# The first 1.5 KB of every row of one value load, fetched by six small loads of their own

## The chip, the cores and the metric

The kernel runs on one core of one Trainium2 chip. The metric is the device time of one execution in microseconds (us). Three runs of the kernel before took 186.15, 186.21 and 186.29 us; the median is 186.21 us. The profile below is of one further execution, which took 186.22 us.

## The reference

One decoding step of grouped attention over a window of a cache. 32 requests (B) have one query token each, with 32 query heads of 128 numbers; 8 key and value heads each serve four query heads. Of 2048 cached positions only the last 512 are used.

```
q = x @ wq                                     # x 32 x 512, wq 512 x 4096
k, v = k_cache[:, :, 1536:, :], v_cache[:, :, 1536:, :]   # 32 x 8 x 512 x 128
p = softmax(q . k / sqrt(128))                 # per request and query head, over 512 positions
o = p . v                                      # 32 x 32 x 128
out = o.reshape(32, 4096) @ wo                 # wo 4096 x 512
```

All inputs are bf16. The parts of the two caches that are read have 33.5 MB each, the two weight matrices 4.2 MB each, so 75.5 MB have to be read for 32 KB of result.

## The kernel before

The 32 requests are worked off in eight quads q of four. One quad's keys are one load of 4 MB: 32 pairs of request and head, each cut into four runs of 128 positions, make 128 rows, one for each partition of the on-chip memory, and each row is one contiguous run of 32 KB in HBM (128 positions of 256 B). The values of a quad are laid out the same way. There are two buffers for keys (`K_sb`) and two for values (`V_sb`); quad q uses buffer q % 2. The weights have no room of their own: `wq` lies in the second value buffer until the queries are made, `wo` in the first key buffer when quad 6 has been transposed.

For each quad VectorE transposes the keys (T, L444, two halves), TensorE makes the scores (S, L331), VectorE and ScalarE make the softmax (M, X, N), TensorE turns the probabilities to the layout of the value rows (E, L346) and ScalarE copies them out (G), VectorE and ScalarE spread them into block-diagonal weights (B), TensorE multiplies them with the values (P, L361), both engines pick the wanted blocks (C), and TensorE folds them (F, L373), which ScalarE copies (D). At the end TensorE multiplies with `wo` (L392) in three parts, as its three loads W0 (16 of 32 column blocks), W1 (12) and W2 (4) come in; VectorE and ScalarE copy the result, and one write of 32 KB ends the program.

The order of the operations on TensorE, VectorE and ScalarE is written out by hand (`PE_OPS`, `DVE_OPS`, `ACT_OPS`); each waits for what `needs` lists. The order of the loads is the list `LOADS`. All of them but those of `x` are issued by SyncE (SP), in this order:

```
K0 K1 V0.0 K2 V1.0 K3 V2.0 K4 V3.0 K5 K6 V4.0 K7 V5.0 V5.1 V6.0 V6.1 V7.0 V7.1 W0 W1 W2
```

The two loads of `wq` come ahead of this list. A load of keys waits until quad q - 2 has been transposed (L227), a load of values until quad q - 2 has been multiplied (L233), V1 until the queries are made (L231). `V_PIECES` says in how many loads a quad's values come: one for quads 0 to 4 and two (V5.0 and V5.1) for 5 to 7. Each load of values adds 16 to a semaphore of its buffer and piece (`sem_v`); `v_waits` (L178) works out what count TensorE has to wait for before it multiplies with a piece, from all loads that have used that semaphore so far.

The four loads of `x` are issued by ScalarE's queue. They have 2, 6, 10 and 14 rows of 1 KB (`X_PARTS`).

## Time and profile before

| what | measured |
|---|---|
| median of three runs | 186.21 us |
| the profiled execution | 186.22 us |
| its span, first to last instruction | 184.4 us |
| outside the span | 1.8 us |
| bytes read, mean rate over the span | 75.53 MB, 410 GB/s |
| TensorE busy (matmul), VectorE busy, ScalarE busy | 119.1, 106.6, 49.9 us |
| SP issues W2, W2 has landed | 157.82, 181.40 us |
| the last matmul has ended, the write is issued | 181.86, 182.53 us |

The profile is a page on one execution; its trace can be asked for more: for the chain of work that ended last, for the waits, for the instructions in a stretch of time, and for the transfers in it. Data come over 16 DMA engines that work beside each other. A load is cut into packets, here one for each row and engine, and each engine that took part in a load adds to the load's semaphore by a 4-byte packet after its last row. The "DMA" row of the page is the mean busy share of the 16 engines in each slice. Queue q1 is SP's, q10 ScalarE's; the "instruction" queues fetch the program itself. The trace also keeps each packet's start, length and size and the time of each semaphore addition, but not the number of the engine that moved it.

### The profile page before, as it was taken

The numbers are of one execution on the slowest core, as the hardware profiler recorded it, in microseconds if no ns is written. First come the engines' busy times: TensorE is split into PE (matmuls) and PEld (weight loads), VectorE is DVE, ScalarE is ACT, GpSimd is POOL, SyncE is SP. The second block draws the span as 40 slices with busy tenths as digits, with TensorE's granted clock in tenths as the row PEclk, the third lists the DMA queues.
The fourth block names the chain that finished last, engine by engine and source line by source line (L and its number), as shares of the span: only waits on it lengthen the run. The fifth ranks groups of instructions, "written<-read, shape, count | busy, mean of one in ns | idle before, by whom it ended". The sixth has DMA issues, their size and how long they took to land.

```text
span 184.4 us, 3662 instructions
## 1 busy us (share of the span) xinstructions
PE 119.1 (65%) x1636; PEld 56.8 (31%) x1636; DVE 106.6 (58%) x106; ACT 49.9 (27%) x93; POOL 16.9 (9%) x52
## 2 busy tenths in 40 slices
PE   0089104448796794549944992441799899988872
PEld 0024000014542451304431450000245445444362
DVE  0032999994549632963298327999636996302031
ACT  3001200011935157001650162001062714502031
POOL 7900040202000200002000200020000000000000
PEclk9999955555599999657987699555579999999999
DMA  6999999989999999998999999999999999999970
GB/s 224 412 508 398 398 455 455 455 384 412 451 455 437 398 409 455 455 430 377 435 451 455 412 405 434 441 448 405 434 430 402 430 426 423 426 419 430 422 314 32
DMA packets 3584, 75.80 MB, mean 411 GB/s; under 512 B 432, under 2 KB 496, under 8 KB 624
## 3 DMA queue, kind: packets, MB, share of 16 engines
q1 hardware_dynamic: 3504, 75.53, 96.1%
q8 instruction: 13, 0.21, 0.5%
q10 hardware_dynamic: 64, 0.03, 0.1%
q14 instruction: 3, 0.02, 0.0%
HBM read 75.53 MB, written 0.03 MB: 410 GB/s over the span
## 4 chain that ended last, share of the span: by engine, by line
DMA 77%; DVE 13%; issue 3%; PE 3%; SPq 3%; DVEq 0%
DMA K_sb<-in_k_cache_dram 49%; DMA V_sb<-in_v_cache_dram 15%; DMA K_sb<-in_wo_dram 13%; DVE KT_sb L444 12%; PE ps L361 2%; SPq L236 1%; SPq L228 1%; SPq L242 1%; PE ps L331 1%; SPq L193 0%; DVE C_sb L469 0%; DVE maxv L450 0%; PE ps L392 0%; DVEq L120 0%; DVE P_bf L478 0%
## 5 line engine op out<-in xcount | busy, mean ns | idle before, releaser
L444 DVE STREAM_TRANSPOSE KT_sb<-K_sb 128x4096 f32<-128x4096 f32 x16 | 70.6, 4433 | 12.5 <-DMA K_sb<-in_k_cache_dram 12.4
L361 PE MATMUL ps<-V_sb,bd 32*128 32x512 bf16 x1024 | 63.3, 397 | 4.6 <-DMA V_sb<-in_v_cache_dram 2.7
L331 PE MATMUL ps<-KT_sb,QBD 128*32 128x512 bf16 x256 | 25.2, 532 | 39.7 <-DVE KT_sb L444 30.1
L361 PEld LDWEIGHTS ps<-V_sb,bd 32*128 32x128 bf16 x1024 | 27.1, 97 | 37.9 <-issue 12.2
L331 PEld LDWEIGHTS ps<-KT_sb,QBD 128*32 128x32 bf16 x256 | 6.6, 114 | 56.1 <-DVE KT_sb L444 37.0
L495 ACT ACTIVATE P_f<-ps,negmax 128x512 f32<-128x512 f32 x8 | 5.5, 687 | 63.2 <-DVE negmax L452 63.2
L508 ACT ACTIVATE bd<-PTc,mask 128x512 bf16<-128x512 bf16 x31 | 20.1, 710 | 0.3
L513 ACT ACTIVATE C_sb<-ps 32x512 f32<-32x512 f32 x22 | 12.9, 588 | 25.5 <-PE ps L361 25.4
L289 POOL COPY QBD<-QT_sb 32x128 bf16<-32x128 bf16 x32 | 9.2, 287 | 106.5 <-PE ps L331 90.3
L464 DVE TENSOR_SCALAR bd<-PTc,mask 128x512 bf16<-128x512 bf16 x33 | 9.4, 349 | 13.9 <-ACT PTc L502 13.9
L469 DVE COPY C_sb<-ps 32x512 f32<-32x512 f32 x10 | 6.9, 692 | 15.6 <-PE ps L361 15.5
L373 PE MATMUL ps<-C_sb,F_sb 128*128 128x128 f32 x64 | 9.7, 299 | 6.4 <-ACT C_sb L513 5.8
L346 PE MATMUL ps<-P_bf,E_sb 128*128 128x128 bf16 x128 | 11.0, 254 | 0.8 <-DVE P_bf L458 0.8
L373 PEld LDWEIGHTS ps<-C_sb,F_sb 128*128 128x128 f32 x64 | 8.2, 201 | 9.4 <-ACT C_sb L513 8.1
L346 PEld LDWEIGHTS ps<-P_bf,E_sb 128*128 128x128 bf16 x128 | 9.3, 116 | 4.9 <-DVE P_bf L458 2.8
L502 ACT ACTIVATE PTc<-ps 128x512 bf16<-128x512 f32 x8 | 4.8, 594 | 18.2 <-PE ps L346 18.1
L450 DVE TENSOR_REDUCE maxv<-ps 128x1 f32<-128x512 f32 x8 | 5.5, 687 | 7.2 <-PE ps L331 7.2
L313 PE MATMUL ps<-V_sb,bd 128*128 128x512 bf16 x32 | 8.6, 435 | 0.8 <-DVE bd L412 0.8
L301 PE MATMUL ps<-bd 32*128 32x128 bf16 x4 | 0.6, 295 | 9.0 <-DMA bd<-in_x_dram 9.0
L412 DVE CAST bd<-ps 128x512 bf16<-128x512 f32 x1 | 0.7, 692 | 9.6 <-PE ps L301 9.6
L433 DVE CAST KT_sb<-ps 128x512 bf16<-128x512 f32 x4 | 2.5, 684 | 6.0 <-PE ps L313 6.0
L489 ACT ACTIVATE KT_sb<-ps 128x512 bf16<-128x512 f32 x4 | 2.1, 602 | 13.8 <-PE ps L313 13.8
(29 smaller groups left out, 33.9 us busy)
## 6 DMA issues: line engine op xcount, KB each, us to landing
K_sb<-in_k_cache_dram SPq DMA_DIRECT2D x8, 4096.0 KB, 25.6
V_sb<-in_v_cache_dram SPq DMA_DIRECT2D x5, 4096.0 KB, 30.0
V_sb<-in_v_cache_dram SPq DMA_DIRECT2D x6, 2048.0 KB, 16.4
V_sb<-in_wq_dram SPq DMA_DIRECT2D x2, 2048.0 KB, 9.8
K_sb<-in_wo_dram SPq DMA_DIRECT2D x1, 2048.0 KB, 19.8
K_sb<-in_wo_dram SPq DMA_DIRECT2D x1, 1536.0 KB, 22.8
K_sb<-in_wo_dram SPq DMA_DIRECT2D x1, 512.0 KB, 23.6
out_dram<-P_bf SPq DMA_DIRECT2D x1, 32.0 KB, 1.5
```

The costliest lines, as they stand in the source:

```text
L289: pool.tensor_copy(QBD[pr, q % 2].rearrange("p (w t) (h c) -> p w t h c", w=2, h=HKV)[:, :, :, :, 4 * b:4 * b + 4], QT_sb[pr, q].rearrange ...
L313: ins = pe.matmul(ps[:, n], lhsT=xT_sb[:, kt, :], rhs=wq_sb[:, kt, n * 512:(n + 1) * 512], start=kt == 0, stop=kt == DKT - 1, tile_positio ...
L331: ins = pe.matmul(S_ps[32 * c:32 * c + 32, :], lhsT=QBD[:, q % 2, 2 * w + t, c0:c0 + 32], rhs=KT_sb[:, w, :, KB * h:KB * h + KB, t], start ...
L346: ins = pe.matmul(EP_ps[:, e * R:(e + 1) * R], lhsT=E_sb[:, k, e].rearrange("p m j -> p (m j)"), rhs=P_bf[:, k * R:(k + 1) * R], start=k = ...
L361: ins = pe.matmul(O_ps[:, b, :], lhsT=bd[pr, q % 2, 4 * g:4 * g + 4].rearrange("p r h e -> p (r h e)"), rhs=V_sb[q % 2][pr, 512 * g:512 * ...
L373: ins = pe.matmul(F_ps[:, 0:P], lhsT=F_sb[:, d].rearrange("p h d -> p (h d)"), rhs=C_sb[:, q % 2, :, 32 * d:32 * d + 32], start=d == 0, st ...
L444: return dve.transpose(KT_sb[:, w].bitcast(F32).rearrange("p r c t -> p r (c t)"), K_sb[q % 2][:, :].bitcast(F32).rearrange("p (r w c) -> ...
L450: dve.tensor_reduce(maxv[:, q:q + 1], S_ps, AX.X, ALU.max).then_inc(s["dve_m"], 1)
L464: ins = dve.tensor_scalar(o, i, m, None, op0=ALU.mult)
L469: ins = dve.tensor_copy(*pick_args(q, r))
L508: ins = act.activation(o, i, ACTF.Copy, scale=m)
L513: ins = act.activation(*pick_args(q, r), ACTF.Copy)
```

## The change

For the second quad (q = 1) the first 6 positions of each row's 128, which are 1.5 KB of its 32 KB, no longer come with the row. They come by six loads of their own, ahead of the row's rest, over the partitions of 6, 6, 6, 6, 5 and 3 pairs of request and head (24, 24, 24, 24, 20 and 12 partitions). The rest of each row, 30.5 KB, is one load over 128 partitions as before. All seven loads add to the same semaphore, so that `v_waits` counts six more for this buffer from quad 1 on. They are issued where V1 stood. The destination, the order of all other operations and the number of bytes are the same.

```diff
 V_PIECES = [1, 1, 1, 1, 1, 2, 2, 2]
+V_HEAD, V_HEAD_R = 1, 6
+V_HEAD_LOADS = [(0, 6), (6, 12), (12, 18), (18, 24), (24, 29), (29, 32)]
@@ v_waits
                     c = sum(1 for p in range(q % 2, q + 1, 2) if V_PIECES[p] > i)
+                    if i == 0 and q >= V_HEAD and q % 2 == V_HEAD % 2:
+                        c += len(V_HEAD_LOADS)
                     yield i * 32 // n, sem_v[q % 2][i], 16 * c
@@ the loads of values, on SP
                     n = R // V_PIECES[q]
-                    r0 = op[2] * n
+                    r0, r1 = op[2] * n, op[2] * n + n
+                    if q == V_HEAD:
+                        r0 = V_HEAD_R
+                        for w0, w1 in V_HEAD_LOADS:
+                            sp.dma_start(
+                                V_sb[q % 2][4 * w0:4 * w1, 0:r0 * DH],
+                                v_cache[4 * q:4 * q + 4, :, SK - W:, :].rearrange(
+                                    "b h (k r) d -> (b h) k (r d)", k=KB)[w0:w1, :, 0:r0 * DH],
+                            ).then_inc(sem_v[q % 2][0], 16)
                     sp.dma_start(
-                        V_sb[q % 2][:, r0 * DH:(r0 + n) * DH], rows(v_cache, q, r0, r0 + n)
+                        V_sb[q % 2][:, r0 * DH:r1 * DH], rows(v_cache, q, r0, r1)
                     ).then_inc(sem_v[q % 2][op[2]], 16)
```

## The prediction

> **What bounds the kernel now.** I read the slices and the queues of the page first, then the chain of work that ended last, then the transfers and the instructions of the last microseconds.

> ```profile
> DMA  6999999989999999998999999999999999999970
> GB/s 224 412 508 398 398 455 455 455 384 412 451 455 437 398 409 455 455 430 377 435 451 455 412 405 434 441 448 405 434 430 402 430 426 423 426 419 430 422 314 32
> q1 hardware_dynamic: 3504, 75.53, 96.1%
> q8 instruction: 13, 0.21, 0.5%
> q10 hardware_dynamic: 64, 0.03, 0.1%
> ```

> The sixteen DMA engines are busy from the first slice to the last but two, at some 425 GB/s. No compute engine comes near that. Each load is also issued well ahead: the tightest, V7.0, is issued at 155.49 us, when the foremost engine still has V6.1 to move until 158.6. So an engine's end is the sum of its packets. The chain's end says the same:

> ```profile
> 157.35 0.43 SPq L242
> 157.78 0.04 issue
> 157.82 23.57 DMA K_sb<-in_wo_dram
> 181.40 0.04 issue
> 181.44 0.42 PE ps L392 x15
> 181.86 0.02 issue
> 181.88 0.28 DVE P_bf L478
> ```

> The last part of `wo`, W2, lands at 181.40 us and 16 matmuls wait for it; from there to the end of the span it is a fixed 3.0 us. What counts is whether all engines end together. They don't. Time by stages, with the share of the sixteen engines that was busy and GB/s in the last two columns:

> ```profile
> 176.00:178.00 2.00, 1.40 (x12) 1.14 (x10) 0.72 (x2) 0.80 (x2) 0.00 (x0) 1.00 0.94 381
> 178.00:179.60 1.60, 1.17 (x65) 0.90 (x64) 0.00 (x0) 0.28 (x1) 0.00 (x0) 1.00 0.48 197
> 179.60:180.80 1.20, 0.60 (x44) 0.60 (x48) 0.00 (x0) 0.00 (x0) 0.00 (x0) 1.00 0.26 106
> ```

> From 179.6 to 180.8 us a quarter of the engines is at work: four, at the same 26.5 GB/s each that they have when all work (425 / 16), so it is the engine that limits and not what they share. The sixteen additions to W2's semaphore agree: twelve come between 178.26 and 180.05 us, then four at 181.19, 181.31, 181.37 and 181.40.

> What makes four late? In the packet records an engine can be followed, since its next packet starts 3 to 4 ns before the last one's end. A 16 KB row takes 607 ns from start to start, but a 16 KB piece of program (queue q8, for TensorE, one every 256 of its instructions) holds its engine for 1.55 us: 1.05 us until the next row starts and 0.5 us by which that row is longer. The pieces go to eight engines in turn, and by the end four engines have carried two: those fetched at 46.3 and 151.2, 57.3 and 161.0, 68.1 and 167.6, 81.5 and 176.7 us. These are the four.

> **Which engines a small load uses.** The loads of `x` have 2 + 6 + 10 + 14 = 32 rows, and q10 shows 64 packets: 32 rows and 32 additions, one for each engine that took part. So a load of n rows ran on n engines. Followed through, six engines carry at least three of these rows, four carry two, four one, two none, as if each load took the first n of one fixed order. Of the four late engines two carry two rows and two carry one. None is among the first six.

> **The change, part by part.**

> 1. The head loads' engines. The source of a head load is walked as 6 (or 5, or 3) heads, in each 4 runs. The rows bound it: 6 rows of `x` went to 6 engines, and loads over 128 partitions, whose source is walked as 32 heads of 4 runs, to all 16. I take the number of heads, 6, 6, 6, 6, 5, 3, by the row that it is nearest to, the 6-row load; the other end, with 24 partitions as the number that is divided, is 12 engines, a rival. [...]

> 2. What it takes off. Rows of 16 KB and 4 KB take 607 and 155 ns, which is 0.0368 ns a byte and 4 ns besides. A row that is 1536 bytes shorter saves 56.5 ns, and each engine has 8 of the 128 rows: 0.45 us off all sixteen, and off the ten beyond the first six for good. The four late ones then bring W2 at 181.40 - 0.45 = 180.95.

> 3. What it adds. A row of 1536 bytes costs 4 + 56.5 = 61 ns by that line, between the 46 ns of a 1 KB row of `x` and the 159 ns of a 4 KB row of W2; I take 61, as the 1 KB row lies on the line (42 ns from start to start). A load over 6 engines gives each 4 such rows. The first three engines get 24 rows and 6 additions of 6 ns: 1.46 + 0.04 - 0.45 = +1.04 us; the fourth and fifth 20 rows, +0.79; the sixth 16 rows, +0.54. Of those six the latest now (it carried one piece of program, at 142.5 us) brings W2 at 180.05, the next at 179.38. With +1.04 the latter comes to 180.42, which is early. The former comes to 180.59 if it is the sixth, 180.84 if the fourth or fifth, both under 180.95; if it is one of the first three, 181.09. The records don't tell which.

> 4. Six more issues on SP, some 0.57 us each by the rows of its 25 (0.37 to 0.62): 3.7 us. They stand where V1 stood, at 32.98 us, so the rest of V1 is issued at 36.7. Behind it SP waits for the transpose that releases K3 (42.23), so nothing behind is later. The engines come to V1 at about 51 us, when K2 is through. Without this cover it would cost 3.7 us.

> 5. V1's arrival. The last addition of V1 comes at 62.98 now, from a late engine, and goes to 62.5 there; the first six come at 61.3 to 61.7, and with +1.04 at 62.7 at most. TensorE starts on it at 63.11, after the scores of quad 3. Nothing waits longer. TensorE's wait counts seven loads instead of one in the same instruction, and its instruction count, and so its program fetches, stay.

> 6. The end. W1 (180.16) is late on the same four engines and moves by 0.45 as well, as does V7.1, on which the matmuls ahead wait. TensorE is idle for 0.67 us ahead of W1 and 0.38 us ahead of W2:

> ```profile
> 178.46 1.08 PE L392 MATMUL ps<-K_sb,o_sel 128*32 128x128 bf16 x64 [0.37 <-ACT o_sel L517]
> 180.20 0.85 PE L392 MATMUL ps<-K_sb,o_sel 128*32 128x128 bf16 x48 [0.67 <-DMA K_sb<-in_wo_dram]
> 181.44 0.43 PE L392 MATMUL ps<-K_sb,o_sel 128*32 128x128 bf16 x16 [0.38 <-DMA K_sb<-in_wo_dram]
> ```

> W0's matmuls end at 179.54 even without any shift and W1 is there at 179.71, so the whole 0.45 us passes to the end.

> The sum: 186.22 (the profiled execution, which is 0.01 us from the median) - 0.45 = 185.77 us, 0.24% less. The measurement tells about 0.2%, 0.37 us, from no change, so this is a narrow "faster".

> **The rivals.**

> A. The engine that brings W2 at 180.05 is one of the first three. Then it is the last, at 181.09, and the gain is 0.31 us: 185.91. For it: three of six places. Against it: nothing but the other three.

> B. The head loads spread over 12, 12, 12, 12, 10 and 12 engines. Then the two late engines in places seven to ten get 11 rows: 0.67 + 0.04 - 0.45 = +0.26 us, so W2 at 181.66 and 186.48 us, within 0.2%. Against it: the 6-row load of `x` on 6 engines.

> C. Slower: a 1.5 KB row costs more than its bytes, on the first three engines at 52 us. The point from which this decides: 180.05 - 0.45 + 24 c is later than 181.40 for c above 75 ns (102 ns if rival A's engine isn't among the three). At 4 KB's 159 ns W2 would come at 183.4 and the run end at 188.2; at 100 ns, at 182.0 and 186.8. For it: the 1 KB rows of the result took 45 to 79 ns. Against it: those run on idle engines with nothing behind them, while the rows of `x`, in a full queue as here, took 44 to 46. [...]

> D. Slower: in the new program the pieces of program go to other engines, and a twice-hit engine is among the first three. Then W2 comes at 181.40 + 1.04 and the run takes 187.26. Against it: TensorE's instructions stay, and three runs within 0.14 us don't look like a draw.

> E. Nothing at all, 186.21: some other thing holds the end.

> **How the numbers follow.** The likeliest gets 0.52 and A 0.25: by places alone they would share evenly, but A needs the row's price as well, since under 55 ns (24 rows: 1.32 + 0.04 - 0.45 = 0.90) its engine comes no later than the four, and the price is only known to lie above the 42 ns of 1 KB. B gets 0.06, C 0.07, D 0.06, E 0.04. Point: 185.77. The range 185.6 to 186.3 holds the likeliest, A and E, 0.81; its low end is the point less the spread of the runs (0.14). Faster by over 0.2%: 0.46 of the likeliest's 0.52, as its margin over that bound is only 0.08 us, and 0.04 of A: 0.50. Slower by over 0.2%: C and D but for their cheap ends, 0.12. Same: the rest, 0.38.

> **What the next profile would show.** If the heads go to 6, 6, 6, 6, 5 and 3 engines, q1 has 128 more rows and 32 more additions: 3664 packets, and 3702 with rival B. If the likeliest holds, W2 lands near 180.9, its last four additions are still those of the same four engines, and the stretch with few engines at work is shorter by 0.45 us. If A: a fifth engine among the last, and W2 near 181.1. If C: head rows over 75 ns in the packet records. If D: the last engines carry head rows. I'd be wrong in the reasoning, too, if a queue ran dry near 52 us because SP issues the rest of V1 late, or if TensorE had no idle time left ahead of W2.

## The result, and the profile after

The changed kernel takes 187.17 us (median of 9 runs, 186.66 to 188.29), the kernel before beside it 186.34 us (9 runs, 186.15 to 186.57). The ratio is 1.0055, with a 95% interval of 1.0032 to 1.0078: 0.55% slower, where 0.24% faster was forecast. The runs also spread over 1.6 us, those of the kernel before over 0.4.

The profiled execution took 186.66 us, the fastest of the nine, with a span of 184.9 us. The slices and the first queue of its page:

```profile
DMA  6998999998999999999999999999999999999981
GB/s 224 411 507 383 411 454 454 454 411 383 450 327 429 446 450 447 411 394 447 448 443 404 418 418 454 447 418 432 408 447 401 418 440 411 433 418 433 415 363 41
q1 hardware_dynamic: 3664, 75.53, 96.4%
```

q1 has 3664 packets in place of 3504: 128 more rows and 32 more additions, as belong to heads on 6, 6, 6, 6, 5 and 3 engines. Slice 12 (50.8 to 55.5 us) has 327 GB/s at a busy share of nine tenths; before, the twelfth slice had 455. That is where the heads run. The end of the chain of work:

```profile
159.36 22.46 DMA K_sb<-in_wo_dram
181.82 0.04 issue
181.87 0.42 PE ps L404 x15
182.28 0.02 issue
182.31 0.28 DVE P_bf L490
```

W2 lands at 181.82 us, 0.42 later than before, and the execution is 0.44 us longer. The loads still set the end. The last stages, with busy share and GB/s of the DMA engines in the last two columns:

```profile
176.00:178.00 2.00, 1.40 (x13) 1.24 (x13) 1.12 (x2) 1.18 (x3) 0.00 (x0) 1.00 0.98 410
178.00:179.60 1.60, 1.23 (x59) 1.04 (x60) 0.00 (x0) 0.28 (x1) 0.00 (x0) 1.00 0.82 333
179.60:180.80 1.20, 0.52 (x37) 0.34 (x28) 0.00 (x0) 0.00 (x0) 0.00 (x0) 1.00 0.48 195
```

In the stage from 179.6 us half of the engines are at work where a quarter was. So work did move to the engines that were early, but the end went the other way.

What happened at 51 to 54 us is seen when 48 to 56 us is taken as one stage, first of the kernel before, then of the changed one:

```profile
48.00:56.00 8.00, 7.41 (x119) 3.77 (x121) 3.87 (x5) 4.24 (x7) 0.00 (x0) 0.82 0.94 406
```

```profile
48.00:56.00 8.00, 6.60 (x96) 3.28 (x97) 3.60 (x8) 4.98 (x9) 0.00 (x0) 0.79 1.00 374
```

The share of busy engines is higher, 1.00 in place of 0.94, and yet they move 374 GB/s in place of 406. The packet records say which packets are long. Head rows take 65 ns at first, as priced, and up to 167 ns later, 94 on average. And the rows behind them, which nobody had priced: on nine of the ten engines without heads the first two rows of V1's rest take 1.4 to 1.7 us in place of 1.16. The tenth was still at its last row of K2, which takes 1.84 us in place of 1.21, and its first row of V1's rest takes 1.41. That is 0.88 us for each of the ten, 0.86 to 0.90, against the 0.45 us that they save: +0.43, which is the 0.42 us of W2. On the six engines with heads the first row behind the heads takes 1.37 to 1.70 us. Of the later rows one alone is long, behind a piece of program. W2's last four additions, from 181.72 us on, come from engines without heads that carried two pieces of program each; the last from an engine with heads comes at 181.46.

SP is not in it. Its issues in this execution (start, length):

```profile
33.61 0.54 SPq L232 DMA_DIRECT2D K_sb<-in_k_cache_dram  x1
34.19 4.81 SPq L243 DMA_DIRECT2D V_sb<-in_v_cache_dram  x6
39.04 0.59 SPq L248 DMA_DIRECT2D V_sb<-in_v_cache_dram  x1
43.05 0.57 SPq L232 DMA_DIRECT2D K_sb<-in_k_cache_dram  x1
```

The six small issues take 0.72 to 0.91 us each, more than the 0.57 that was taken for them, but the rest of V1 is issued 12 us before the engines come to it, and K3 is issued when its transpose is done.

### The profile page after: what moved, and what is told of

Read it like the earlier page. It is cut to its first block, busy times and chain, and to the rows that moved or that the text cites. A ratio compares the mean times of both kernels' runs of the same rounds, so it can differ in the third digit from the quotient of the medians.

```text
span 184.9 us, 3668 instructions
## 1 busy us (share of the span) xinstructions
PE 119.6 (65%) x1636; PEld 55.9 (30%) x1636; DVE 106.5 (58%) x106; ACT 49.7 (27%) x93; POOL 16.9 (9%) x52
## 3 DMA queue, kind: packets, MB, share of 16 engines
q1 hardware_dynamic: 3664, 75.53, 96.4%
HBM read 75.53 MB, written 0.03 MB: 409 GB/s over the span
## 4 chain that ended last, share of the span: by engine, by line
DMA 64%; DVE 21%; PE 8%; issue 3%; SPq 2%; ACTq 1%; DVEq 0%
DMA K_sb<-in_k_cache_dram 33%; DVE KT_sb L456 16%; DMA V_sb<-in_v_cache_dram 15%; DMA K_sb<-in_wo_dram 12%; PE ps L325 4%; DMA bd<-in_x_dram 4%; PE ps L373 2%; DVE QT_sb L448 2%; DVE KT_sb L445 1%; SPq L248 1%; ACTq L191 1%; SPq L254 1%; PE ps L343 1%; DVE bd L424 0%; DVE C_sb L481 0%
## 5 line engine op out<-in xcount | busy, mean ns | idle before, releaser
L373 PE MATMUL ps<-V_sb,bd 32*128 32x512 bf16 x1024 | 64.5, 404 | 4.9 <-DMA V_sb<-in_v_cache_dram 2.3
L507 ACT ACTIVATE P_f<-ps,negmax 128x512 f32<-128x512 f32 x8 | 5.5, 684 | 62.7 <-DVE negmax L464 62.7
L385 PE MATMUL ps<-C_sb,F_sb 128*128 128x128 f32 x64 | 9.2, 287 | 7.1 <-ACT C_sb L525 6.5
L358 PE MATMUL ps<-P_bf,E_sb 128*128 128x128 bf16 x128 | 9.8, 238 | 0.9 <-DVE P_bf L470 0.9
L325 PE MATMUL ps<-V_sb,bd 128*128 128x512 bf16 x32 | 9.7, 479 | 0.8 <-DVE bd L424 0.8
L358 PEld LDWEIGHTS ps<-P_bf,E_sb 128*128 128x128 bf16 x128 | 8.4, 108 | 4.8 <-DVE P_bf L470 2.7
```

The costliest lines, as they stand in the source:

```text
L325: ins = pe.matmul(ps[:, n], lhsT=xT_sb[:, kt, :], rhs=wq_sb[:, kt, n * 512:(n + 1) * 512], start=kt == 0, stop=kt == DKT - 1, tile_positio ...
L358: ins = pe.matmul(EP_ps[:, e * R:(e + 1) * R], lhsT=E_sb[:, k, e].rearrange("p m j -> p (m j)"), rhs=P_bf[:, k * R:(k + 1) * R], start=k = ...
L373: ins = pe.matmul(O_ps[:, b, :], lhsT=bd[pr, q % 2, 4 * g:4 * g + 4].rearrange("p r h e -> p (r h e)"), rhs=V_sb[q % 2][pr, 512 * g:512 * ...
L385: ins = pe.matmul(F_ps[:, 0:P], lhsT=F_sb[:, d].rearrange("p h d -> p (h d)"), rhs=C_sb[:, q % 2, :, 32 * d:32 * d + 32], start=d == 0, st ...
```

## The experiments

All times are medians with the range of the runs; the kernel before, beside them, took 186.33 us (186.14 to 186.81, 25 runs) in the first series, 186.40 (186.16 to 186.93, 24 runs) in the second, 186.43 (186.18 to 186.96, 28 runs) in the third and 186.34 (186.08 to 186.88, 19 runs) in the fourth. Where an edit is told as "in place of", it starts from the changed kernel.

### What slows the rows: size, source or destination

**e1_one_load.** The same cut, but the heads come by one load over the same 128 partitions as the rest of the rows, so that each engine is taken to bring the heads of its own rows.

```diff
-V_HEAD_LOADS = [(0, 6), (6, 12), (12, 18), (18, 24), (24, 29), (29, 32)]
+V_HEAD_LOADS = [(0, 32)]
```

> The rows of V1 are cut at 1.5 KB as in the changed kernel, but the heads come by one load over all 128 partitions, in place of six over 24 and fewer. In the changed kernel's profile the head rows take 65 to 167 ns (94 on average, 61 were forecast) and the first two of the rows that follow, on the ten engines without heads, 1.4 to 1.7 us in place of 1.16. Three theories. Way-in theory: a group of partitions takes data in no faster than one engine brings them, and rows that another engine brings there are taken from the group's own engine. Here each engine brings its own, so head rows 65 ns, all following rows 1.16 us, 16 more rows and additions of 5 ns: 186.2 to 186.4 us, as before. Source theory: the heads all begin at multiples of 32 KB in HBM and meet in one place there, which holds up all engines. Then the slow rows are here again, with sixteen engines on it at once: 186.7 us or more. Size theory (rival C of the prediction): a 1.5 KB row costs 100 ns and more by its size; then 8 rows on each engine take 0.4 us more: 186.6 us, and the rows that follow are not slowed.

Measured: 186.42 us (186.29 to 186.73), ratio 1.0004 (0.9995 to 1.0014). All 128 head rows take 65 to 67 ns, and but for the one that a piece of program prolongs, the rows behind them 1.16 us. The stage from 48 to 56 us keeps its 406 GB/s:

```profile
48.00:56.00 8.00, 7.42 (x111) 3.64 (x112) 3.87 (x5) 4.19 (x7) 0.00 (x0) 0.77 0.96 406
```

So it isn't the size, nor the place that the heads have in HBM, from which they come here as well.

**e2_other_source.** The same six loads from another place in HBM.

```diff
-                                v_cache[4 * q:4 * q + 4, :, SK - W:, :].rearrange(
-                                    "b h (k r) d -> (b h) k (r d)", k=KB)[w0:w1, :, 0:r0 * DH],
+                                wq.rearrange("k n -> (k n)")[0:32 * 5 * 832].rearrange(
+                                    "(a k f) -> a k f", k=5, f=832)[w0:w1, 0:KB, 0:r0 * DH],
```

> The six head loads as in the changed kernel, same partitions and engines, but read from the query weights, in rows of 1.5 KB that lie 1664 bytes apart, so that they don't meet at multiples of 32 KB. The values of those positions are wrong by that; the work is the same. Way-in theory: as the changed kernel, head rows over 100 ns from the second load on and rows of 1.4 to 1.7 us behind them, 186.7 to 188 us. Source theory: both gone, the predicted gain appears, 185.8 to 186.0 us. Size theory: head rows over 100 ns, the others 1.16 us.

Measured: 187.00 us (186.55 to 187.96), ratio 1.0047 (1.0027 to 1.0066), as the changed kernel. Head rows up to 139 ns, and the rows behind them are slow as in the changed kernel (1.42 to 1.74 us, 0.85 to 0.87 us for each of the ten engines). The source doesn't matter.

**e3_rows_own, e8_rows_mid and e4_rows_far.** The same source rows, but other destinations: the second key buffer, which is free from the transpose of quad 1 until K3.

```diff
                     if q == V_HEAD:
                         r0 = V_HEAD_R
+                        wait([ends["T", 1, 1]])
...
-                                V_sb[q % 2][4 * w0:4 * w1, 0:r0 * DH],
+                                K_sb[1][0:4 * (w1 - w0), w0 // 5 * r0 * DH:(w0 // 5 + 1) * r0 * DH],
...
+                    if q == 3:
+                        sp.wait_ge(sem_h, 16 * len(V_HEAD_LOADS))
```

e8 has partitions from 32 on, e4 from 96 on, in place of 0. The heads add to a semaphore of their own (sem_h). The first 1.5 KB of each row of V1 are left out by this, as the heads don't reach the value buffer.

> The six head loads with the same source rows, but each writes partitions 0 to 23 (0 to 19, 0 to 11) of the second key buffer, which is free at that time, side by side; so each of the six engines brings all its rows to one group of four partitions, taken to be its own. They are issued after the second half of the transpose of quad 1 (42.2 us), and K3 waits for them. The first 1.5 KB of V1 are left out by this: the buffer keeps older bytes there. Way-in theory: no engine brings rows to another's partitions, so head rows 61 to 65 ns, all rows behind them 1.16 us, and the gain that was predicted: 185.8 to 185.95 us. Source theory and size theory: as the changed kernel, 186.7 to 188 us, head rows over 100 ns.

> As e3_rows_own, but partitions 32 to 55 (32 to 51, 32 to 43) are written by the six loads. In e4_rows_far all ten engines without heads were slowed, not only those that fill partitions 96 to 119. If each engine fills two groups of four partitions of a full load, and the second of the first six engines lie here (a second way-in of their own), nothing is held up: head rows 65 ns, 185.8 to 187 us. If only partitions 0 to 23 are theirs, it is as in e4_rows_far: head rows over 100 ns on average, first rows behind them 1.4 to 1.9 us on ten engines, 187 to 189 us.

> As e3_rows_own, but the six loads write partitions 96 to 119 (96 to 115, 96 to 107), so that the six engines bring all their rows to partitions that are others' to fill. The first 1.5 KB of V1 are left out in the same way. Way-in theory: the engines that fill these partitions, six of the ten without heads at the most, get 12 to 24 rows of others in place of 8, so they are slowed by 1 to 3 us and the other engines without heads not at all; if a late engine is among them, 187 to 189 us. Source theory: all ten are slowed alike, as in the changed kernel, 186.7 to 188 us. Size theory: head rows over 100 ns, the ten not slowed.

Measured: e3 186.17 us (185.83 to 188.19), ratio 1.0004 (0.9979 to 1.0029); e8 186.00 (185.68 to 187.73), ratio 0.9999 (0.9971 to 1.0026); e4 188.16 (187.14 to 189.19), ratio 1.0097 (1.0068 to 1.0125). The same stage in e3, e8 and e4, in this order:

```profile
48.00:56.00 8.00, 7.40 (x113) 3.80 (x114) 3.82 (x5) 4.43 (x8) 0.00 (x0) 0.78 0.99 422
```

```profile
48.00:56.00 8.00, 7.42 (x120) 3.83 (x121) 3.93 (x5) 4.30 (x8) 0.00 (x0) 0.84 0.97 414
```

```profile
48.00:56.00 8.00, 6.75 (x100) 3.20 (x104) 2.23 (x5) 4.19 (x7) 0.00 (x0) 0.79 0.95 328
```

With partitions 0 to 23 or 32 to 55 nothing is held up (422 and 414 GB/s, head rows 66 ns on average), with 96 to 119 more than in the changed kernel (328 GB/s, head rows 112 ns, first rows behind them 1.74 to 1.98 us). Destination decides: e4 differs from e3 and e8 in nothing but the partitions. And where it is harmless, the gain that was forecast is there: the profile of e3 is one of 185.83 us, with W2 landing at 181.01, 0.39 earlier than before, and its last four additions from engines without heads. It is the fastest of e3's ten runs, whose median is no better than before; why they spread is taken up below.

```profile
181.01 0.04 issue
181.05 0.42 PE ps L406 x15
```

Which engine fills which partition in a full load stands in no record. That 0 to 23 are the six engines' own was the author's assumption in e3 and e4, and two groups of four for each engine that in e8. The runs give an estimate: each engine brings 8 of the 128 rows of a full load, so six engines fill 48 partitions, and 0 to 23 and 32 to 55, where e3 and e8 held up nothing, are 48. By this estimate, which no run shows directly, partitions are called the six engines' own here and below, and all others those that they don't fill.

By this estimate the way-in theory was right on the place, but it was wrong on who pays. It wanted only those engines slowed whose partitions are taken, in e4 six of the ten at most by its own count. All ten were, by about 1.33 us each.

One thing isn't separated. The harmless heads went to partitions that the six engines fill themselves, and these all lie below 64; the harmful ones to partitions that the six don't fill, and most of these lie from 64 up. That partitions from 64 up are slow by themselves is out, since in e1 all 128 rows take 65 to 67 ns, theirs among them. That they are slow only for the first six engines is not. e14 (below) speaks against it: there, too, 64 of the 128 rows go to partitions from 64 up, but 88 in place of 80 to partitions that no engine with heads fills (at 8 rows an engine, five fill 40 of the 128 and six 48), and each engine without heads loses 1.00 us, where the profiles with 80 rows (the changed kernel, e2, e5 and e9) have 0.80 to 0.90.

**e12_after_half.** Half the bytes in as many rows.

```diff
-V_HEAD, V_HEAD_R = 1, 6
+V_HEAD, V_HEAD_R = 1, 3
```

> The changed kernel with heads of 768 bytes in place of 1536 (V_HEAD_R 3), the same six loads and partitions, nothing left out. The ten engines without heads lost 0.88 us each to 80 head rows that went to partitions other than 0 to 23 and 32 to 55, and in e4_rows_far about 1.35 us to 128: 11 ns a row in both. By rows: 0.88 us again, with half the gain: +0.88 - 0.23 = +0.65 us on the late engines, 186.85 us at best. By bytes: 0.44 - 0.23 = +0.21 us, 186.4 us at best.

Measured: 186.96 us (186.28 to 187.23), ratio 1.0024 (1.0009 to 1.0039); its fastest run is at 186.28, that of e9, e2 and the changed kernel at 186.55 to 186.66. Summed over all engines, the rows behind the heads and the head rows themselves lost 5.3 us, in the changed kernel 14.3 and in e4 21.3 (length over 1188 or 1160 ns for a row of the rest, over 36 or 65 ns for a head row, for rows that start before 55.5 us). The bytes that went to partitions that none of the six engines fills, by the estimate above 80, 80 and 128 rows, are 61, 123 and 197 KB. So the loss goes with the bytes and not with the rows: 0.09 to 0.12 us of engine time a KB, where bringing a KB takes 0.04.

### What spreads the runs

**e5_after_again, e6_own_again, e7_own_again2.** The changed kernel and e3 again, for other profiles.

> The changed kernel once more, for another profile: its runs spread from 186.7 to 188.3 us where those of the kernel before lie within 0.7 us. Pieces theory (rival D of the prediction): which engines carry two pieces of program differs from run to run; before the change that makes no difference, since all engines have the same rows, but now six have more. Then a profile of 187.3 us or more has two pieces on an engine with head rows, which is the last, and one of 186.9 or less has not. Cross theory: the pieces' engines stay, and what varies is how much the head rows hold up each other and the rows behind them (0.9 us per engine without heads in the first profile); then a slower profile shows slower rows at 51 to 54 us.

> e3_rows_own once more, for another profile. There the head rows hold up nobody, but ten runs still spread from 185.83 to 188.19 us. Pieces theory: a profile at 186.7 us or more has its last additions from an engine with head rows that carried two pieces of program; one at 185.8 to 186.1 has not. Cross theory: no spread is explained here, as there are no slow rows at 51 to 54 us.

> The same as e6_own_again, a third profile, with the same expectations: the more runs, the likelier a slow one is among the profiles.

Measured: 187.79 us (187.18 to 187.96, 4 runs), ratio 1.0070 (1.0050 to 1.0090); 186.50 (185.97 to 187.32), ratio 1.0007 (0.9989 to 1.0025); 186.57 (186.04 to 187.08), ratio 1.0013 (0.9999 to 1.0026). None of the three profiles is of a run a microsecond above the others. They showed two smaller things. In e5, e6 and e4 TensorE stands still in the middle of its last matmuls. Of e5:

```profile
180.79 0.74 PE L404 MATMUL ps<-K_sb,o_sel 128*32 128x128 bf16 x40 [0.68 <-DMA K_sb<-in_wo_dram]
182.12 0.53 PE L404 MATMUL ps<-K_sb,o_sel 128*32 128x128 bf16 x24 [0.58 <-issue]
```

It waits for nothing that the profile shows, and the twelfth piece of program was fetched at 179.7 us there (179.1 in e6, 180.3 in e4), at 177.2 in the first profile of the changed kernel. That TensorE waits for this piece is argued from these times. And in e6 the edit itself disturbs: its heads wait for the transpose, so that V1's rest was issued at 48.25 us, and some first rows of it took 2.6 and 2.9 us on engines without heads; in e3 and e7, issued at 47.31 and 47.96, none did.

**e9_after_short, e10_before_short, e11_mid_short.** So that TensorE's program ends before that point, the last quarter of its final matmuls is left out of the changed kernel, of the kernel before and of e8.

```diff
-                        for c in cs:
+                        for c in [c for c in cs if c < 3]:
```

> The changed kernel without a quarter of the matmuls with wo (the fourth of the four column blocks, 32 of 128 matmuls; the last 128 columns of the result are left out by this). All loads stay. In the profiles at 186.5, 187.18 and 187.69 us TensorE stands idle for 0.58 to 0.85 us after the 40th matmul of W1, with no wait in the program, and the twelfth piece of program was fetched at 179.1 to 180.3 us; in the profiles at 185.8 to 186.7 us it was fetched at 176.2 to 177.6 and there is no such gap. Late-piece theory: the spread of the changed kernel (186.66 to 188.29) is from this wait. TensorE's program is shorter by 64 instructions here and ends before the point where it stood idle, so the runs should lie within 0.6 us, at 186.4 to 186.9. Other theories of the spread (the amount by which the head rows hold others up, or engines with heads that carry two pieces of program): 186.5 to 188.3 as before.

> The same quarter of matmuls left out of the kernel before, as the base for e9_after_short. Late-piece theory: its runs lie from 186.14 to 186.93 us, few of them with the wait; without it 186.0 to 186.4. The difference of the medians of e9 and this one is then what the held up rows cost alone: +0.88 - 0.45 us, 0.43. Other theories: no change in its spread.

> The same quarter of matmuls left out of e8_rows_mid (heads to partitions 32 to 55, the first 1.5 KB of V1 left out), where nothing is held up and yet the runs lie from 185.68 to 187.73 us. Late-piece theory: 185.6 to 186.1 us. If engines with heads that carry two pieces of program make the spread, it stays: up to 1.04 us over the kernel before, 187.3.

Measured: e9 187.68 us (186.58 to 188.47), ratio 1.0050 (1.0027 to 1.0073); e10 186.36 (186.27 to 186.59), ratio 0.9994 (0.9985 to 1.0004); e11 186.01 (185.84 to 186.94), ratio 0.9991 (0.9973 to 1.0008). The late-piece theory falls for the large part: e9 and e11 spread as before, in two groups. e9 has four runs at 186.58 to 186.82 and six at 187.64 to 188.47; e11 six at 185.84 to 186.03 and four at 186.78 to 186.94. Only the kernel before became narrower (186.27 to 186.59), and no faster that could be told.

e11's profile is one of its upper group (186.92 us) and shows what the group is. The transfers from 176 to 184 us in 40 slices:

```profile
DMA  8999799969769762442412100000000000000000
GB/s 369 430 532 410 307 471 389 389 266 389 307 287 389 328 266 102 184 184 82 184 61 82 41 20 41 20 20 20 0 0 0 0 0 0 0 0 0 0 0 0
```

From 180.6 us on there are 20 to 40 GB/s, one packet of 4 KB in 0.2 us or two: a single engine. Fifteen additions of W2 have come by 180.99, the last at 182.09. Followed back, this engine has 16 head rows, so it is the sixth, and carried the pieces of program fetched at 81.1 and 176.5 us. In the profiles of e3 and e8, both of runs of the lower group, the sixth carried one, at 135.8 and at 132.1 us.

**e13_mid_five, e14_after_five.** e11 and e9 with the heads on five engines.

```diff
-V_HEAD_LOADS = [(0, 6), (6, 12), (12, 18), (18, 24), (24, 29), (29, 32)]
+V_HEAD_LOADS = [(0, 5), (5, 10), (10, 15), (15, 20), (20, 25), (25, 30), (30, 32)]
```

> As e11_mid_short (heads to partitions 32 to 55, the first 1.5 KB of V1 and the last 128 columns of the result left out), but with seven loads over the partitions of 5, 5, 5, 5, 5, 5 and 2 heads, so that five engines bring all heads and the sixth none. e11 had two groups of runs, 185.84 to 186.03 and 186.78 to 186.94 us, and its profile, of the second group, ends with the sixth engine, the one of 16 head rows, which carried two pieces of program (at 81.1 and 176.5 us); in the profiles of e3 and e8, at 185.83 and 185.75 us, the sixth carried one. Turn theory: the eight engines that take pieces are always the sixth and seven without heads, and what differs from run to run is which of them comes first. Then nothing of the second group is left: all runs at 185.8 to 186.2 us. If any engine can take pieces, or the second group has another cause, runs at 186.8 us and more stay, since the first two engines now have 28 head rows, +1.26 us.

> The same seven loads in the changed kernel's own partitions (e9_after_short with five engines for heads; the last 128 columns of the result left out). e9 had runs at 186.58 to 186.82 and at 187.64 to 188.47 us. Turn theory: only the first group stays, and the rows that go to other engines' partitions, 88 in place of 80, cost every engine 0.97 us in place of 0.88: 186.6 to 187.0 us. Otherwise runs over 187.5 us stay.

Measured: e14 186.87 us (186.69 to 187.18, 10 runs), ratio 1.0029 (1.0020 to 1.0039): the upper group is gone. e13 185.87 us (185.65 to 187.64), ratio 0.9978 (0.9956 to 1.0000): eight runs at 185.65 to 186.02, none at 186.8 to 187, and two outside, at 186.56 and 187.64. The first of the two is the profiled one, and it has the disturbance of e6: with seven loads ahead of it V1's rest is issued at 48.71 us, where e3 had 47.31. SP's issues of e13, then of e3:

```profile
43.21 5.46 SPq L245 DMA_DIRECT2D K_sb<-in_v_cache_dram  x7
48.71 0.59 SPq L250 DMA_DIRECT2D V_sb<-in_v_cache_dram  x1
```

```profile
42.47 4.80 SPq L245 DMA_DIRECT2D K_sb<-in_v_cache_dram  x6
47.31 0.58 SPq L250 DMA_DIRECT2D V_sb<-in_v_cache_dram  x1
```

What the run at 187.64 us was is open; it has no profile.

So the larger part of the spread of the changed kernel is the sixth engine's turn: whether it comes among the first four of the eight that take pieces, and so has two of the twelve by the end, or later and has one. By four places of eight half of the runs would be in the upper group; e9 had six of ten and e11 four. Seen directly it is in e11's profile alone; that it holds for e9 and the changed kernel rests on e14, where the sixth has no heads and the group is gone. In the lower group the last engines are others, and the run costs what the held up rows cost, 186.65 by the sum above, 186.66 measured. In the upper group the sixth is last: in e9's packet records its 16 head rows take 1.40 us and its slow first row 0.46 more, less the saved 0.45, so about +1.4 us on an engine with two pieces: 187.6, an estimate from these rows, and the group begins at 187.64. No run was found that beats the kernel before with the whole result.

## Why the prediction was wrong, by its steps

Bound and end (the first part, and step 6): right. The end moved with W2 in each profile that was compared, by +0.42 us here and -0.39 in e3, and all of it passed to the end.

Step 1, the engines of a head load: right, by the 3664 packets. Rival B is out: its 12 engines were an estimate, an even split of 24 rows as the loads before had even splits (2, 6, 10 and 14 rows on as many engines, 128 on sixteen), and no run shows a load that ran so.

Step 2, the 0.45 us saved on each engine: right. Rows of 30.5 KB take 1.16 us where nothing disturbs, against 1.21, and e3's profile has the gain.

Step 3 failed, in the price of a head row and in what it was charged to. The 61 ns hold in e1, e3 and e8 (65 ns long, 61 from start to start) and not here, with 94 on average. The rows that the price came from, those of `x`, lacked neither the place in a full queue nor the destination: they go to partitions 0 to 31, and of the ten that came on ten engines to partitions 8 to 17, at least four came on engines beyond the first six, to partitions that by the estimate above the six fill. What they lacked is number, 2 to 14 rows of 1 KB at a time. In e4, too, the first 31 head rows, 48 KB in 0.4 us, still took 65 to 67 ns, and only those behind them were held up. Rival C had a dearer row, but as a matter of size, and e1 shows that size costs nothing. That its sum comes near is chance: at 94 ns it puts W2 at 180.05 - 0.45 + 24 x 0.094 = 181.86 us on an engine with heads, and 181.82 was measured, but on engines without. The larger part had no term at all: the sum treated the engines as independent, so that a row moved to an early engine is free for the late ones. It cost each of them 0.88 us.

Rival A's question, which of the six is the one at 180.05, has an answer: followed through the profiles that tell it, the one engine of the six that carries pieces of program is always the sixth. In the changed kernel's profile its last addition comes at 181.46, where step 3 had 180.59 for the sixth. What isn't fixed is whether it carries one piece or two.

Rival D was put down to 0.06 by an argument that can't carry it. The pieces of program do go to the eight engines in another turn from run to run. The three runs within 0.14 us were no evidence against that: in the kernel before all engines bring the same bytes, so it makes no difference who has two pieces. The change gave six engines more to bring, and one of them is among the eight.

Steps 4 and 5: right that nothing waits for SP; the issues are longer than priced and hidden. V1's last addition comes at 63.50 us in place of 62.98, later than the 62.7 that was forecast, again by the slow rows.

What fell is the assumption that the engines are independent of each other; the mechanism of the gain and its size stood, as e3 shows (W2 0.39 us earlier, where 0.45 was forecast).

## What to carry to other kernels

Where the engines' packets set the end, as here, moving rows to an engine that is early can cost more than it saves: here the rows that six engines brought to partitions other than 0 to 23 and 32 to 55 held up all sixteen, by 0.09 to 0.12 us of engine time a KB, where bringing a KB takes 0.04. Test such a move first with other destinations: e3 and e4 differ in nothing else, and took 186.17 and 188.16 us. A price for a small transfer has to come from rows with the same destination pattern and from as many of them in a stretch, not only from a row of like size: 61 ns were priced by size, and the head rows took 94. And the narrow spread of the balanced kernel, three runs within 0.14 us, said nothing about what is drawn anew in each run, here the engines that carry two pieces of program: ask which draws a spread can't show.
